# Score tiles of an attention kernel made by four 32x32 products instead of one 32x128 product

## The chip, the cores and the metric

The kernel runs on one core of one Trainium2 chip. Five engines work side by side on it: TensorE (PE, matrix products, with its weight loads shown as PEld), VectorE (DVE), ScalarE (ACT), GpSimd (POOL) and SyncE (SP, which issues the DMAs). The metric is the device time of one execution in microseconds. The kernel before takes 734.96 us, the median of three runs from 733.4 to 735.26 us.

A product on PE has a stationary operand, which a weight load puts into the array, and a moving operand that streams through it. A row of the profile gives the part of the array that a product uses as rows*columns: "32*128" has 32 rows of contraction and 128 output partitions, "128*21" has 128 rows and 21 output partitions. A product that uses less than the whole array is given a position in it (`tp`, a row and a column), and products at different positions can run at the same time. Products write to PSUM, which has eight banks of 128 partitions x 512 float32.

## The reference, cut to what matters

Two blocks of the same size stand side by side, S = 2048 rows, D = 640, 32 heads of 20 elements. Block A is softmax attention, block B is linear attention; their outputs are concatenated.

```
# A
scores = einsum("bhqd,bhkd->bhqk", q, k) * 20 ** -0.5
p = softmax(scores)
o = einsum("bhqk,bhkd->bhqd", p, v);  a = o @ wo
# B
phi(t) = where(t > 0, t + 1, exp(t)) + 1e-6
kv = einsum("bhsd,bhse->bhde", phi(k), v);  z = sum_s phi(k)
o = (phi(q) @ kv) / (phi(q) @ z + 1e-6);  b = o @ wo
out = concat(a, b)
```

The change touches only `scores` of block A.

## The kernel before, in words

**Tiling.** A unit of block A's work is a pair of a chunk of 512 queries and a group of four heads, 32 units in all (`od`). The four heads of a group lie in four strips of 32 partitions (20 elements of a head, a row for a constant, the rest unused) of `f_KT` (keys) and `f_Qr` (queries). For a unit, a block of 128 keys `kt` and a head `i` of the group, one product makes a score tile, 128 keys x 512 queries, in one PSUM bank: contraction over the 32 partitions of strip `i`, 128 output partitions. There are 32 x 16 x 4 = 2048 such tiles.

**What becomes of a tile.** Most tiles go in pairs to ACT, which takes the exponential of two banks with one instruction (L1832) and writes `f_PT`. The others go one by one to DVE, which clamps and converts them to 16-bit integers in `f_Sr` (L1730); these bits are read as bfloat16 numbers, and POOL moves them on by a constant with an integer add (L1903) twice, so that three slightly shifted approximations of the exponential are summed. The next products, of `f_PT` or `f_Sr` with the values `f_V` (or `f_Vp`, scaled), accumulate the attention output: four heads at a time, each a product of 128 rows and 21 columns at its own column position, one "quad".

**Banks.** Two pairs of banks, (0, 1) and (2, 3), take the tiles for ACT in turn; bank 4 accumulates the output (`PVB`); banks 5, 6 and 7 serve everything else: the tiles for DVE, the projections of block A and all of block B.

**Order of the work.** The whole program is written out by a planner before it runs. `_Fast.run` keeps a free time for each engine and a time at which each buffer is ready, and always lets the engine that is free first take its next step. For PE, `try_pe` tries in this order: a score burst (`try_burst`), a step of a projection or of block B that is under way, a quad of attention outputs (`try_pv`), a burst of tiles for DVE alone (`d_burst`), another step, and a small product on zeros as a filler. A score burst holds the two tiles of the next ACT instruction and, when the planner wants one and a bank is free, one tile for DVE, in rare cases two; the tiles of a burst for different heads lie in different row strips of the array. Only the last product of a burst raises the semaphore.

**Costs in the planner.** `burst` adds the given duration to PE's free time, and 107 ns (`SW`) whenever the kind of burst changes: "R" is a score burst, "C" a quad of products with 128 rows and at most 32 columns, "F" a transpose on the whole array. A score burst is given 219 ns, a quad of 512 columns 217 ns. Steps of block B are let in by the share of score bursts already placed (`pace`, `frac`). So these durations decide the order of the instructions on every engine, but not how long the chip takes for them.

**Where the diff acts.** `score_mm` makes the description of the product; `try_burst` and `d_burst` collect the tiles and hand them to `burst`. All of PE's products but the transposes are recorded at line L156, so the profile tells them apart by their tiles.

Of the kernel before, what the change touches and what calls it, by code (L numbers as in the profile page):

```python
# [769 lines left out]
class _Fast:  # L770
# [911 lines left out]

    def score_mm(self, n, kt, i, b):
        g = self.od[n][1]
        return dict(out=self.ps[:, b, :], l=self.KT[32 * i:32 * i + 32, g, 128 * kt:128 * (kt + 1)],
                    r=self.Qr[32 * i:32 * i + 32, n % 4, :], start=True, stop=True,
                    reads=self.kres(n, kt, i), writes=(("ps", b),), tp=(32 * i, 0))

    def scored(self, n):
        self.scnt[n] = self.scnt.get(n, 0) + 1  # L1690
# [52 lines left out]
    def try_burst(self, t):  # L1743
        if self.jS >= len(self.groups):
            if self.dS < len(self.dq) and self.abank:
                return self.d_burst(t)
            return False
        j = self.jS
        if j > self.jE + 1:
            return False  # L1750
        grp = self.groups[j]
        for u, n, kt, i in grp:
            if not self.kready(n, kt):
                return False
        bs = self.SB[j % len(self.SB)]
        mms = [self.score_mm(n, kt, i, bs[k]) for k, (u, n, kt, i) in enumerate(grp)]
        rd = [r for m in mms for r in m["reads"]]
        wr = [r for m in mms for r in m["writes"]]
        if self.est("pe", rd, wr) > t + 30:
            return False  # L1760
        rows = set(g[3] for g in grp)
        post = []
        want = self.dlead() < self.DLEAD and self.dfl < self.DMAX
        slack = self.free["act"] - t - 560
        if want:
            b = min(self.abank, key=lambda x: self.est("pe", (), (("ps", x),))) if self.abank else None
            pd = self.pick_d(rows, t)
            if pd is not None and (b is None or self.est("pe", (), (("ps", b),)) > t + 30):
                if slack > 0 and self.ready_c(t):
                    return False  # L1770
                pd = None
            if pd is not None:
                mm, ps_ = self.take_d(pd[0], pd[1], b)
                mms.append(mm)
                post.append(ps_)
                rows.add(pd[1])
                if self.dlead() < self.DOUBLE and self.abank and self.dfl < self.DMAX:
                    b = min(self.abank, key=lambda x: self.est("pe", (), (("ps", x),)))
                    pd = self.pick_d(rows, t) if self.est("pe", (), (("ps", b),)) <= t + 30 else None
                    if pd is not None:  # L1780
                        mm, ps_ = self.take_d(pd[0], pd[1], b)
                        mms.append(mm)
                        post.append(ps_)
        for u, n, kt, i in grp:
            self.scored(n)
        self.burst("R", mms, 219.0)
        for f in post:
            f()
        self.jS += 1
        self.q["act"].append(self.exp_op(j))  # L1790
        return True
# [4 lines left out]
    def d_burst(self, t):  # L1796
        mms, post, rows = [], [], set()
        for b in list(self.abank):
            if self.est("pe", (), (("ps", b),)) > t + 30:
                continue  # L1800
            pd = self.pick_d(rows, t)
            if pd is None:
                break
            mm, p = self.take_d(pd[0], pd[1], b)
            rows.add(pd[1])
            mms.append(mm)
            post.append(p)
        if not mms:
            return False
        self.burst("R", mms, 219.0)  # L1810
        for f in post:
            f()
        return True
# [510 lines left out]
```

## Time and profile before

| What | Value |
|---|---|
| Median of three runs | 734.96 us |
| Profiled execution, its own time | 732.96 us |
| Span of the profiled execution | 731.2 us |
| PE busy | 712.0 us, 11241 products |
| ACT busy | 694.5 us, 784 instructions |
| DVE busy | 636.9 us |
| POOL busy | 340.9 us |
| Granted PE clock, mean | 0.998 |

The busy time of PE is the union of the time from the start of each product to its modelled end. Products are pipelined: a product of 512 columns shows about 0.38 us, but the next one at the same position starts after some 0.22 us. So the distance between starts, in the timeline, tells more about PE than its busy time. A row of a timeline gives the start in us, the length in us from the first start to the last end, the engine, the line, the operation and its tiles, the array part and the moving operand, and how many instructions are merged in it. "The chain of waits" is the chain of work that ended last, followed back from the end of the span.

### The profile page before, as it was taken

How to read it: one execution, taken by the hardware profiler on the slowest of the kernel's cores; microseconds unless marked ns; L12 is line 12 of the kernel's file. 1: busy time of each engine (PE TensorE's matmuls, PEld its weight loads, DVE VectorE, ACT ScalarE, POOL GpSimd, SP SyncE). 2: the span in 40 equal slices, each digit the busy share in tenths (PEclk: the TensorE clock that was granted, in tenths of full speed). 3: DMA queues.
4: the chain of work that ended last, by engine and by line, in shares of the span. 5: the costliest groups of instructions: out<-in, count | busy, mean ns of one | idle time of the engine just before them, and what ended most of it. 6: DMA issues, size and time to landing. Idle time of an engine off the chain costs nothing.

```text
span 731.2 us, 25772 instructions
## 1 busy us (share of the span) xinstructions
PE 712.0 (97%) x11241; PEld 253.3 (35%) x11241; DVE 636.9 (87%) x1181; ACT 694.5 (95%) x784; POOL 340.9 (47%) x331
## 2 busy tenths in 40 slices
PE   8999999999999999999999999999999999999997
PEld 5323434333223333333333333323323333332333
DVE  6898888988888988898999998899889899898993
ACT  4799898999999999999999999999999999999994
POOL 7644444545554554342554443654441554424442
PEclk9999999999999999999999999999999999999999
DMA  8511011006200100102001000302102001000001
GB/s 200 157 29 35 13 33 37 13 9 151 59 10 29 32 12 18 34 4 37 20 17 34 18 9 5 101 6 47 38 15 66 23 21 35 9 27 24 6 20 59
DMA packets 42608, 27.64 MB, mean 38 GB/s; under 512 B 26890, under 2 KB 41930, under 8 KB 42490
## 3 DMA queue, kind: packets, MB, share of 16 engines
q1 hardware_dynamic: 41178, 25.62, 13.4%
q8 instruction: 89, 1.46, 0.8%
q10 hardware_dynamic: 1312, 0.33, 0.2%
q14 instruction: 29, 0.24, 0.1%
HBM read 8.40 MB, written 5.24 MB: 19 GB/s over the span
## 4 chain that ended last, share of the span: by engine, by line
PE 53%; ACT 33%; DVE 9%; POOL 1%; DMA 1%; issue 1%; SPq 0%; DVEq 0%; POOLq 0%; ACTq 0%
PE ps L156 53%; ACT f_PT L1832 32%; DVE f_Sr L1730 4%; ACT f_ar L1383 1%; POOL f_Sr L1903 1%; DVE f_T L1923 1%; DVE f_ar L1385 1%; DMA f_ar<-in_A_wqkv_dram 1%; DVE f_T L1930 1%; PE ps L1002 1%; DVE f_ar L1387 1%; DVE f_sq L1211 0%; DVE f_OTn L1927 0%; DVE f_xT L1161 0%; DVE f_Rt L1921 0%
## 5 line engine op out<-in xcount | busy, mean ns | idle before, releaser
L1832 ACT ACTIVATE f_PT<-ps 128x1024 bf16<-128x1024 f32 x724 | 681.0, 1090 | 22.7 <-PE ps L156 21.7
L1903 POOL INT64_ADD f_Sr<-f_Sr x300 | 317.4, 1067 | 370.0 <-PE ps L156 314.7
L1730 DVE TENSOR_SCALAR f_Sr<-ps 128x512 int16<-128x512 f32 x600 | 404.8, 683 | 64.1 <-PE ps L156 57.8
L156 PE MATMUL ps<-f_Qr,f_KT 32*128 32x512 bf16 x2048 | 291.7, 385 | 6.4 <-ACT f_PT L1832 3.0
L156 PEld LDWEIGHTS ps<-f_Qr,f_KT 32*128 32x128 bf16 x2048 | 73.9, 91 | 248.2 <-ACT f_PT L1832 204.6
L156 PE MATMUL ps<-f_ar 128*32 128x320 bf16 (+4 forms) x3024 | 150.1, 295 | 1.1 <-DVE f_Sr L1730 0.5
L156 PE MATMUL ps<-f_PT,f_V 128*21 128x512 bf16 x1448 | 137.2, 382 | 1.3 <-issue 1.3
L156 PE MATMUL ps<-f_Sr,f_V 128*21 128x512 bf16 x1200 | 111.0, 382 | 2.6 <-POOL f_Sr L1903 2.2
L156 PEld LDWEIGHTS ps<-f_ar 128*32 128x32 bf16 x3024 | 60.9, 95 | 61.6 <-issue 35.3
L156 PE MATMUL ps<-f_Sr,f_Vp 128*21 128x512 bf16 x600 | 58.9, 383 | 0.1
L156 PEld LDWEIGHTS ps<-f_PT,f_V 128*21 128x21 bf16 x1448 | 35.5, 90 | 42.3 <-issue 35.1
L156 PEld LDWEIGHTS ps<-f_Sr,f_V 128*21 128x21 bf16 x1200 | 28.6, 90 | 38.7 <-issue 20.0
L156 PE MATMUL ps<-f_ar,f_xT 128*32 128x160 bf16 x1280 | 34.9, 234 | 0.7 <-DMA f_ar<-in_A_wqkv_dram 0.7
L987 DVE CAST f_st<-ps 128x320 bf16<-128x320 f32 x60 | 28.3, 476 | 7.5 <-PE ps L156 7.5
L1923 DVE TENSOR_TENSOR f_T<-f_T,f_Rt 128x512 bf16<-128x512 f32 x32 | 34.3, 1071 | 0.2
L156 PE MATMUL ps<-f_wo,f_OTd 128*32 128x320 bf16 (+1 forms) x608 | 31.3, 302 | 0.0
L1383 ACT ACTIVATE f_ar<-ps 128x320 bf16<-128x320 f32 (+1 forms) x52 | 31.0, 597 | 0.0
L156 PE MATMUL ps<-f_xT,f_ar 128*32 128x512 bf16 x400 | 30.6, 382 | 0.1
L1387 DVE SCALAR_TENSOR_TENSOR f_ar<-ps,f_ar 128x320 bf16<-128x320 f32 (+1 forms) x52 | 28.8, 554 | 0.5
L156 PEld LDWEIGHTS ps<-f_ar,f_xT 128*32 128x32 bf16 x1280 | 22.9, 96 | 14.9 <-issue 9.3
L1385 DVE TENSOR_SCALAR f_ar<-f_ar 128x320 bf16<-128x320 bf16 (+1 forms) x52 | 23.3, 448 | 4.7 <-ACT f_ar L1383 3.8
L1930 DVE STREAM_TRANSPOSE f_T<-ps 128x512 f32<-128x512 f32 x32 | 22.6, 707 | 3.5 <-PE ps L156 3.5
(70 smaller groups left out, 291.1 us busy)
## 6 DMA issues: line engine op xcount, KB each, us to landing
out_dram<-f_st SPq DMA_DIRECT2D x32, 160.0 KB
f_ar<-in_B_wqkv_dram SPq DMA_DIRECT2D x3, 800.0 KB
f_OTd<-f_OTn SPq DMA_DIRECT2D x105, 20.0 KB
f_Qr<-f_sq SPq DMA_DIRECT2D x88, 20.0 KB
f_KT<-f_ar SPq DMA_DIRECT2D x22, 80.0 KB
f_ar<-in_A_wqkv_dram SPq DMA_DIRECT2D x2, 800.0 KB
f_wq<-in_A_wqkv_dram SPq DMA_DIRECT2D x1, 800.0 KB
f_wo<-in_A_wo_dram SPq DMA_DIRECT2D x1, 800.0 KB
```

The source lines that it names most:

```text
L156: lambda e: e.matmul(out, lhsT, rhs, start=start, stop=stop, tile_position=tp, skip_group_check=sgc),
L987: (lambda e: e.tensor_copy(sl, ps[:, b, 0:320])), (("ps", b),), (("stage", s, h),),
L1002: self.sch.op("pe", lambda e, m=m: e.transpose(m["out"], m["in"], m["id"]), reads=m["reads"], writes=m["writes"], inc=m.get("inc", k == le ...
L1383: self.push("act", lambda e: e.activation(r1, src, AF.Exp), (("ps", b),), (rk,), _c_act(n), prio=0, ok=ok, after=lambda: self.push("dve", ...
L1385: "dve", lambda e: e.tensor_scalar(r1, r1, 1.0, 1e-6, op0=ALU.min, op1=ALU.add), (rk,), (rk,),
L1387: "dve", lambda e: e.scalar_tensor_tensor(dst, src, 0.0, r1, op0=ALU.max, op1=ALU.add),
L1730: post = lambda: self.push("dve", lambda e: e.tensor_scalar(self.Sr[:, s, i, :], self.ps[:, b, :], 0.0, 32639.0 - self.PH[-1], op0=ALU.max ...
L1832: return _Op("act", lambda e: e.activation(self.PT[:, s0:s0 + n, :], ps[:, b0:b0 + n, :], AF.Exp, scale=math.log(2.0) / 128.0, bias=self.l ...
L1903: self.q["pool"].append(_Op("pool", lambda e: e.int64_add(v, v, inc), res, res, self.C64, self.C64 + 150, 0, self.seq, after))
L1923: "dve", lambda e: e.tensor_tensor(T2v, Tv, R.unsqueeze(2).broadcast_to([128, 16, 32]), op=ALU.mult),
L1930: self.push("dve", lambda e: e.transpose(self.T[:], ps[:, b, :]), (("ps", b),), ("T",), 630, prio=-1, after=freed, ok=lambda: n == 0 or (" ...
```

## The change

The product of a tile, 32 rows x 128 columns, is split into four of 32 rows x 32 columns. Product `j` has keys 32j to 32j+31 of the block as its weights, sits at row 32i and column 32j of the array, and writes partitions 32j to 32j+31 of the same bank. The moving operand is the same for all four. `weave` puts the products of a burst in order: first `j` = 0 of every tile, then `j` = 1 of every tile, and so on. So the 2048 products and weight loads of the scores become 8192 of each. Buffers, banks, waits between engines and all other products stay as they are. The planner is told 208 + 14 ns for each tile of the burst in place of 219 ns (222, 236, 250 and 264 ns for one to four tiles), and 107 ns for a change of kind as before; the whole order is planned anew with these numbers.

```
     def score_mm(self, n, kt, i, b):
         g = self.od[n][1]
-        return dict(out=self.ps[:, b, :], l=self.KT[32 * i:32 * i + 32, g, 128 * kt:128 * (kt + 1)],
-                    r=self.Qr[32 * i:32 * i + 32, n % 4, :], start=True, stop=True,
-                    reads=self.kres(n, kt, i), writes=(("ps", b),), tp=(32 * i, 0))
+        return [dict(out=self.ps[32 * j:32 * j + 32, b, :],
+                     l=self.KT[32 * i:32 * i + 32, g, 128 * kt + 32 * j:128 * kt + 32 * j + 32],
+                     r=self.Qr[32 * i:32 * i + 32, n % 4, :], start=True, stop=True,
+                     reads=self.kres(n, kt, i), writes=(("ps", b),), tp=(32 * i, 32 * j)) for j in range(4)]
+
+    @staticmethod
+    def weave(tiles):
+        return [m for x in zip(*tiles) for m in x]
...
-        rd = [r for m in mms for r in m["reads"]]
-        wr = [r for m in mms for r in m["writes"]]
+        rd = [r for x in mms for r in x[0]["reads"]]
+        wr = [r for x in mms for r in x[0]["writes"]]
...
-        self.burst("R", mms, 219.0)
+        self.burst("R", self.weave(mms), 208.0 + 14.0 * len(mms))
...
-        self.burst("R", mms, 219.0)
+        self.burst("R", self.weave(mms), 208.0 + 14.0 * len(mms))
```

## The prediction

> **What bounds the kernel now.** I read the busy times and the chain of waits first, then the busy time of each engine by stretch, then the chain in order of time.
>
> ```profile
> PE 712.0 (97%) x11241; PEld 253.3 (35%) x11241; DVE 636.9 (87%) x1181; ACT 694.5 (95%) x784; POOL 340.9 (47%) x331
> ...
> PE 53%; ACT 33%; DVE 9%; POOL 1%; DMA 1%; issue 1%; SPq 0%; DVEq 0%; POOLq 0%; ACTq 0%
> ```
>
> Two engines are nearly full, and the chain changes between them. The busy time by stretch says where each is full (columns: stretch, its length, then PE, PEld, DVE, ACT, POOL busy, the granted clock and DMA):
>
> ```profile
> 0.00:60.00 60.00, 56.62 (x945) 23.96 (x949) 47.78 (x90) 45.49 (x51) 35.38 (x35) 1.00 0.51 126
> 60.00:173.00 113.00, 112.52 (x2096) 42.55 (x2092) 97.12 (x171) 106.78 (x116) 53.67 (x51) 1.00 0.10 23
> 173.00:300.00 127.00, 123.00 (x1755) 40.90 (x1752) 113.00 (x196) 126.36 (x145) 62.23 (x60) 1.00 0.18 44
> 300.00:680.00 380.00, 375.25 (x5704) 126.88 (x5692) 342.11 (x643) 375.88 (x432) 172.19 (x170) 1.00 0.10 27
> 680.00:732.00 52.00, 44.65 (x772) 19.02 (x764) 36.92 (x84) 39.98 (x46) 17.41 (x17) 0.97 0.09 30
> ```
>
> From 60 to 173 us PE alone sets the pace: 0.48 us idle, while ACT idles 6.2. From 173 to 300 it is ACT (0.64 us idle, PE 4.0). From 300 to 680 both are full: PE idles 4.75 us, ACT 4.1. The granted clock is 1.00 up to 680 us, so PE can't be sped up by its clock. The chain in order of time (start, length, what) agrees:
>
> ```profile
> 69.31 63.19 PE ps L156 x1196
> 202.00 45.17 ACT f_PT L1832 x49
> 414.63 31.95 PE ps L156 x522
> ```
>
> So work that is added to PE is paid in full in the second stretch, hidden in the third as far as PE idles there, and paid in the fourth beyond 4.75 us.
>
> **The change part by part.** The rows of the groups count the tiles:
>
> ```profile
> L1832 ACT ACTIVATE f_PT<-ps 128x1024 bf16<-128x1024 f32 x724 | 681.0, 1090 | 22.7 <-PE ps L156 21.7
> L1730 DVE TENSOR_SCALAR f_Sr<-ps 128x512 int16<-128x512 f32 x600 | 404.8, 683 | 64.1 <-PE ps L156 57.8
> L156 PE MATMUL ps<-f_Qr,f_KT 32*128 32x512 bf16 x2048 | 291.7, 385 | 6.4 <-ACT f_PT L1832 3.0
> ```
>
> 724 exponentials of two tiles and 600 tiles for DVE make the 2048 products, so a score burst comes once per exponential, with 2048/724 = 2.8 tiles. Now one stretch of the timeline:
>
> ```profile
> 303.32 0.39 PE L156 MATMUL ps<-f_Qr,f_KT 32*128 32x512 bf16 x3
> 303.64 0.40 PE L156 MATMUL ps<-f_Sr,f_V 128*21 128x512 bf16 x4
> 303.65 0.10 PEld L156 LDWEIGHTS ps<-f_PT,f_V 128*21 128x21 bf16 x4
> 303.86 0.39 PE L156 MATMUL ps<-f_PT,f_V 128*21 128x512 bf16 x4
> 304.18 0.39 PE L156 MATMUL ps<-f_Qr,f_KT 32*128 32x512 bf16 x2
> ```
>
> From one quad to the next it is 0.22 us (303.64 to 303.86), but 0.32 us from the burst to the quad (303.32 to 303.64) and 0.32 us from a quad to the burst (303.86 to 304.18). So each change between the two kinds costs 0.10 us, twice per burst, and three tiles at three row strips cost no more than two.
>
> *The products.* The 512 columns of a tile still stream once; the four parts of a tile run together, like the four products of a quad. What is added is the time until the last of them has started. The products of a quad show how close together such starts are:
>
> ```profile
> 300.54 0.11 PEld L156 LDWEIGHTS ps<-f_Sr,f_V 128*21 128x21 bf16 x8 [0.23 <-issue]
> ...
> L156 PEld LDWEIGHTS ps<-f_Sr,f_V 128*21 128x21 bf16 x1200 | 28.6, 90 | 38.7 <-issue 20.0
> ```
>
> Eight weight loads, interleaved with products, take 0.11 us together where one takes 0.09 us: 0.02/7, about 3 ns from pair to pair. A tile gets three pairs more, so 9 ns; a burst of three gets 27 ns; 2048 tiles get 18.4 us of PE time. Bounds: below, 0, if the added starts overlap entirely; above, the densest supply of short products,
>
> ```profile
> 505.69 0.51 PE L156 MATMUL ps<-f_ar 128*32 128x147 bf16 x24
> 506.03 0.42 PE L156 MATMUL ps<-f_PT,f_V 128*21 128x512 bf16 x4
> ```
>
> 24 pairs in 0.34 us, 14 ns each, 43 ns per tile, 87 us in all. That row is filled by its 147 columns and not by the starts, so I stay at the first, which is a release after a change of kind just like the burst's. The Trainium skill ("TensorE: Matmul & The Clock Gate", section "Measured speedup vs the span model") gives some 4 ns per further tile of the array; by that estimate the added time would be 24.6 us, and by the same sum as below the kernel would take about 750 us; the trace's 3 ns is a little under it.
>
> *The weight loads.* 6144 more, each for 32 columns. They stand in the 3 ns of the pair. Loads of the next quad start 0.01 us after the products of the last one (303.65 against 303.64), so loads don't wait for products of the same rows; without this cover a burst would pay as in the fourth rival.
>
> *The change of kind.* A burst before differs from a quad in rows and columns, one after only in rows (32 against 128). What a change in one of the two costs is seen at the transposes, which use 128 rows and 128 columns:
>
> ```profile
> 503.69 0.45 PE L1002 MATMUL ps<-f_id,f_ar 128*128 128x128 bf16 x5
> 504.07 0.40 PE L156 MATMUL ps<-f_Sr,f_Vp 128*21 128x512 bf16 x4
> ...
> 520.56 0.45 PE L1002 MATMUL ps<-f_id,f_ar 128*128 128x128 bf16 x5
> 520.94 0.39 PE L156 MATMUL ps<-f_Qr,f_KT 32*128 32x512 bf16 x2
> ...
> L1002 PE MATMUL ps<-f_id,f_ar 128*128 128x128 bf16 x100 | 9.7, 222 | 0.0
> ```
>
> Five transposes take 0.45 us and one 0.222, so their pitch is 0.23/4 = 0.057 us and five stream for 0.285 us. To the next burst (only the rows change) and to the next quad (only the columns change) it is 0.38 us: 0.095 us over, both times, as much as where both change. So I leave both changes of a burst at 0.10 us. Bounds: as dear as now, or nothing, which is the first rival.
>
> *Waits.* None is added. Behind the burst's first round of products (`j` = 0 of each tile) stand three more, so if the bank of the DVE tile comes late, the rest of the ACT tiles is late with it; but the semaphore was raised by the burst's last product before too. ACT gets each burst 27 ns later. That is covered by the other pair of banks, whose exponential runs 0.92 us (45.17/49 in the chain); uncovered, 724 x 27 ns is 20 us, the same time as PE's and not to be added to it.
>
> *Supply of instructions.* 12288 more on PE. Priced by the queue that brings them:
>
> ```profile
> span 731.2 us, 25772 instructions
> ...
> q8 instruction: 89, 1.46, 0.8%
> ```
>
> Some 48% more instructions are about 43 packets. A packet takes 0.8% x 16 x 731.2 / 89 = 1.05 us, so uncovered they cost 45 us; but the 89 of now would be 94 us, and PE idles 19 us in all for any reason, so they are fetched ahead. I take 0.
>
> *The sum.* Where the tiles lie, by the same view for the instructions on the keys alone (the number of products stands behind PE's busy time):
>
> ```profile
> 0.00:60.00 60.00, 17.57 (x132) 4.40 (x132) 3.21 (x4) 12.96 (x7) 1.00 0.51 126
> 60.00:173.00 113.00, 46.78 (x328) 12.26 (x328) 0.00 (x0) 0.00 (x0) 1.00 0.10 23
> 173.00:300.00 127.00, 53.06 (x395) 13.30 (x392) 0.00 (x0) 0.00 (x0) 1.00 0.18 44
> 300.00:680.00 380.00, 157.91 (x1091) 39.72 (x1091) 0.00 (x0) 0.00 (x0) 1.00 0.10 27
> 680.00:732.00 52.00, 16.39 (x105) 4.19 (x105) 0.00 (x0) 0.00 (x0) 0.97 0.09 30
> ```
>
> At 9 ns per tile: first stretch 1.2 us, half of it paid, since PE waits there early on for loads: 0.6. Second: 3.0, all paid. Third: 3.6 against PE's idle 4.0: 0. Fourth: 9.8 less 4.75 idle: 5.1. Last: 0.9, 0.6 of it on the chain. Together 9.3 us. The chain's share of PE gives nearly the same, 0.53 x 18.4 = 9.8 us. So 732.96 + 9.3 = 742.3 us against the profiled execution; the median of the runs is 2.0 us above that, so I forecast 744 us. The case's own range: 739 us if the fourth stretch hides everything, 754 us if nothing is hidden (735 + 18.4). The new order of the whole program, planned for bursts of 236 and 250 ns, lies inside it.
>
> **The rivals.**
>
> *1. The change of kind gets cheaper, and the kernel faster.* Burst and quad now both sit on 32 columns, and no row shows a 32*32 product beside a 128*32 one. With 1448 changes, 18.4/1448 = 13 ns less per change is where the cost is even; at nothing left, PE would gain 145 us and ACT would bound throughout. Then the idle time of ACT goes: 6.2 us in the second stretch, 4.1 in the fourth, 0.64 in the third and perhaps 2 of the 14.5 at the start, 13 us: 722 us. Against it: the two transposes' rows above. The Trainium skill ("TensorEngine Tiling (Array Packing)", section "Key Properties") says that changing the tiling mode, and not just the tile, drains the array; by that the 0.10 us stays.
>
> *2. Hidden anyway.* If ACT and DVE hold the pace in the fourth stretch and a good order absorbs the second, 735 us. For it: ACT is 99% busy in both long stretches, and 19 us of PE's span is idle. Against: PE has 0.48 us idle in 113 us of the second.
>
> *3. Supply of instructions or starts fall behind.* At the upper bound per pair, 14 ns, 735 + 87 = 822 us; with the fetch uncovered, 735 + 45 + 9 = 789 us. Against it are the short products that run at 14 ns today, and PE's small idle time.
>
> *4. Loads that wait for products of their own rows.* Four rounds of a burst would follow each other, three more of 0.22 us for 724 bursts: 478 us, 1213 us. The Trainium skill ("TensorE: Matmul & The Clock Gate", section "The mechanism") says that a weight load overlaps products in flight only in another row group. The trace disagrees: the loads at 303.65 are for all 128 rows, and start under products in those rows.
>
> **How the numbers follow.** A measurement of this kernel tells some 0.3% from no change, 2.2 us. Forecast 68%, rival 1 14%, rival 2 12%, rival 3 4%, rival 4 2%. Faster is rival 1, same is rival 2, slower the rest, 74%. The range takes the forecast's own and rival 2 with its spread, 731 to 755 us; outside lie rivals 1, 3 and 4, 20%.
>
> **What would show it.** From the first product of a burst to the next quad: 0.32 us grows to about 0.34 to 0.35 for three tiles; 0.25 or less is rival 1, 0.45 or more rival 3, 0.98 rival 4. PE's idle time from 300 to 680 us should shrink and ACT's grow, by some 5 us; the second stretch should last about 3 us longer for the same 328 tiles. The chain should show PE over 53%. The forecast is wrong if ACT's idle time falls, or if the changes of kind cost something else than 0.10 us.

## The result and the profile after

The changed kernel takes 760.03 us, median of four runs, against 734.79 us before (four runs, one more than in the table above): a ratio of 1.0341, 95% interval 1.0306 to 1.0377. It is slower, as forecast, but by about 25 us and not by 9; 760 lies outside the range of 731 to 755. The profiled execution has a span of 755.2 us.

The burst itself does nearly what the prediction says. These are rows of the timeline of the changed kernel, and its group of score products:

```profile
303.00 0.42 PE L156 MATMUL ps<-f_Qr,f_KT 32*32 32x512 bf16 x12
303.35 0.61 PE L156 MATMUL ps<-f_xT,f_wqp 128*32 128x512 bf16 x8
303.90 0.42 PE L156 MATMUL ps<-f_Qr,f_KT 32*32 32x512 bf16 x12
...
L156 PE MATMUL ps<-f_Qr,f_KT 32*32 32x512 bf16 x8192 | 312.2, 384 | 5.5 <-ACT f_PT L1837 2.3
```

From a burst of three tiles to the next quad it is 0.35 us (303.00 to 303.35), where it was 0.32, and from the quads back to a burst the change of kind still costs some 0.1 us (303.35 to 303.90 for two quads of 0.22). All score products together are busy for 312.2 us where it was 291.7: 20.5 us more, close to the 18.4 that were forecast.

PE's share of the chain grows from 53% to 60%; that it would grow was forecast. What was not foreseen is where the time shows. The chain's shares, and the busy time in the same stretches as in the prediction (columns as there: stretch, its length, PE, PEld, DVE, ACT, POOL):

```profile
PE 60%; ACT 27%; DVE 8%; POOL 2%; DMA 1%; issue 1%; SPq 0%; DVEq 0%; POOLq 0%; ACTq 0%
...
60.00:173.00 113.00, 112.54 (x3020) 44.88 (x3016) 95.78 (x168) 103.41 (x113) 49.24 (x47) 1.00 0.11 24
173.00:300.00 127.00, 122.86 (x2768) 40.62 (x2752) 112.07 (x184) 124.05 (x140) 65.73 (x63) 1.00 0.19 40
300.00:680.00 380.00, 375.64 (x8744) 130.29 (x8734) 330.98 (x606) 376.23 (x428) 169.84 (x169) 1.00 0.11 28
680.00:756.00 76.00, 67.03 (x1570) 33.24 (x1570) 55.70 (x136) 46.55 (x57) 19.28 (x18) 0.99 0.10 33
```

From 300 to 680 us PE idles 4.36 us (4.75 before) and ACT 3.77 us (4.12 before): next to nothing was absorbed there, and ACT was not held up. After 680 us ACT is busy for 46.55 of 76 us. The end of ACT's timeline says why, first of the kernel before, then of the changed one:

```profile
705.93 13.86 ACT L1832 ACTIVATE f_PT<-ps 128x1024 bf16<-128x1024 f32 x15 [0.44 <-PE ps L156]
724.55 1.08 ACT L986 CAST f_st<-ps 128x320 bf16<-128x320 f32 x3 [4.77 <-PE ps L156]
```

```profile
700.05 22.41 ACT L1837 ACTIVATE f_PT<-ps 128x1024 bf16<-128x1024 f32 x24
726.52 0.75 ACT L986 CAST f_st<-ps 128x320 bf16<-128x320 f32 x2 [4.06 <-PE ps L156]
731.08 0.60 ACT L1383 ACTIVATE f_ar<-ps 128x512 bf16<-128x512 f32 x1 [3.81 <-PE ps L156]
...
735.46 0.60 ACT L1383 ACTIVATE f_ar<-ps 128x512 bf16<-128x512 f32 x1 [0.48 <-PE ps L156]
749.78 0.43 ACT L986 CAST f_st<-ps 128x320 bf16<-128x320 f32 x1 [13.73 <-PE ps L156]
```

The last exponential of block A ends at 719.8 us before (705.93 + 13.86) and at 722.5 us after (700.05 + 22.41): 2.7 us later. But five activations of block B (L1383; two of the five rows are shown) come behind it, and the kernel ends 32.7 us after the last exponential, not 11.4 us after it. Cut there, the changed kernel has these two stretches:

```profile
0.00:722.50 722.50, 709.82 (x16740) 255.31 (x16740) 619.40 (x1115) 691.38 (x775) 341.06 (x331) 1.00 0.15 37
722.50:755.20 32.70, 25.41 (x670) 18.68 (x662) 23.11 (x66) 4.59 (x9) 0.00 (x0) 0.99 0.18 60
```

670 products stand in the second stretch. In the kernel before it is 178:

```profile
0.00:719.80 719.80, 705.89 (x11071) 248.84 (x11075) 632.14 (x1168) 692.99 (x780) 340.74 (x331) 1.00 0.14 37
719.80:731.20 11.40, 6.16 (x178) 4.47 (x170) 4.78 (x13) 1.51 (x4) 0.15 (x1) 0.88 0.19 66
```

So nearly all of the loss, 21.3 of the 24.0 us between the two spans, is a part of block B that is left over when block A's scores are done, with ACT and POOL all but idle beside it.

### The profile page after: what moved, and what is told of

Read it like the earlier page. It is cut to its first block, busy times and chain, and to the rows that moved or that the text cites. A ratio compares the mean times of both kernels' runs of the same rounds, so it can differ in the third digit from the quotient of the medians.

```text
span 755.2 us, 38073 instructions
## 1 busy us (share of the span) xinstructions
PE 735.2 (97%) x17402; PEld 274.0 (36%) x17402; DVE 642.5 (85%) x1181; ACT 696.0 (92%) x784; POOL 341.1 (45%) x331
## 4 chain that ended last, share of the span: by engine, by line
PE 60%; ACT 27%; DVE 8%; POOL 2%; DMA 1%; issue 1%; SPq 0%; DVEq 0%; POOLq 0%; ACTq 0%
PE ps L156 60%; ACT f_PT L1837 26%; DVE f_Sr L1735 3%; POOL f_Sr L1908 2%; DVE f_T L1928 1%; DVE f_ar L1385 1%; DMA f_ar<-in_A_wqkv_dram 1%; ACT f_ar L1383 1%; DVE f_T L1935 1%; DVE f_ar L1387 0%; PE ps L1002 0%; DVE f_ar L1565 0%; DVE f_st L987 0%; DVE f_OTn L1932 0%; DVE f_rd L1563 0%
## 5 line engine op out<-in xcount | busy, mean ns | idle before, releaser
L156 PE MATMUL ps<-f_Qr,f_KT 32*32 32x512 bf16 x8192 | 312.2, 384 | 5.5 <-ACT f_PT L1837 2.3
L156 PEld LDWEIGHTS ps<-f_Qr,f_KT 32*32 32x32 bf16 x8192 | 92.9, 87 | 249.6 <-ACT f_PT L1837 219.1
L156 PE MATMUL ps<-f_ar 128*32 128x320 bf16 (+4 forms) x3024 | 145.5, 295 | 3.0 <-DVE f_ar L1387 1.2
L156 PE MATMUL ps<-f_PT,f_V 128*21 128x512 bf16 x1448 | 134.9, 382 | 0.3 <-ACT f_PT L1837 0.2
L156 PEld LDWEIGHTS ps<-f_ar 128*32 128x32 bf16 x3024 | 63.6, 95 | 61.5 <-issue 33.0
L1383 ACT ACTIVATE f_ar<-ps 128x320 bf16<-128x320 f32 (+1 forms) x52 | 28.8, 553 | 5.8 <-PE ps L156 5.8
L1928 DVE TENSOR_TENSOR f_T<-f_T,f_Rt 128x512 bf16<-128x512 f32 x32 | 32.0, 1000 | 0.2
L156 PEld LDWEIGHTS ps<-f_ar,f_xT 128*32 128x32 bf16 x1280 | 22.6, 96 | 14.6 <-issue 10.2
L156 PE MATMUL ps<-f_xT,f_wq 128*32 128x512 bf16 x320 | 25.6, 384 | 0.0
```

Source lines behind the costliest of these rows:

```text
L156: lambda e: e.matmul(out, lhsT, rhs, start=start, stop=stop, tile_position=tp, skip_group_check=sgc),
L1383: self.push("act", lambda e: e.activation(r1, src, AF.Exp), (("ps", b),), (rk,), _c_act(n), prio=0, ok=ok, after=lambda: self.push("dve", ...
L1928: "dve", lambda e: e.tensor_tensor(T2v, Tv, R.unsqueeze(2).broadcast_to([128, 16, 32]), op=ALU.mult),
```

## The experiments

Two things changed at once: what the chip executes per burst, and the order of the whole program, since the planner was told other durations. Theory C: the longer bursts on the chip are what costs. Theory P: the order planned for them costs. Each can be had without the other. The kernel before ran again beside each set of experiments, at 733.02, 733.19 and 733.33 us; each difference below is against the one of its set.

**The new products in the old order.** The planner is told 219 ns as before, so all engines keep the order of the kernel before. The edit stands in both places where a score burst is handed over.

```
-        self.burst("R", self.weave(mms), 208.0 + 14.0 * len(mms))
+        self.burst("R", self.weave(mms), 219.0)
```

> The four 32x32 products per tile, but the planner is told 219 ns per burst as before, so every engine's order is that of the kernel before. Theory P (the new order, laid out for longer bursts, is what costs more than the prediction's 9 us, because it puts block B behind the last exponentials): with the old order only what PE's idle time cannot hide is paid, 742 to 747 us. Theory C (the chip's longer bursts are paid in full under any order, because PE's idle time hides nothing): 735 plus some 20 us, 752 to 758 us. Both expect 0.35 us from the first product of a three-tile burst to the next quad.

Measured: 744.53 us, ratio 1.0158 (1.0141 to 1.0175), +11.5 us. The chain, the score products, and the stretches up to the last exponential and behind it:

```profile
PE 80%; DVE 7%; ACT 6%; POOL 4%; issue 1%; DMA 1%; ACTq 0%; DVEq 0%; POOLq 0%
...
L156 PE MATMUL ps<-f_Qr,f_KT 32*32 32x512 bf16 x8192 | 310.6, 384 | 4.9 <-ACT f_PT L1837 2.4 <-DVE f_Sr L1735 1.7
...
0.00:730.90 730.90, 719.30 (x17207) 265.31 (x17211) 634.24 (x1168) 699.02 (x780) 340.52 (x331) 1.00 0.15 38
730.90:742.60 11.70, 6.40 (x186) 4.52 (x174) 4.79 (x13) 1.56 (x5) 0.39 (x1) 0.95 0.21 74
```

Here the time goes where the prediction looked for it. Score products are busy 18.9 us more (310.6 against 291.7), the last exponential comes 11.1 us later, the stretch behind it is as short as before, and PE bounds nearly all of the way, 80% of the chain. So in the old order the products cost 11.5 us, not 20, and theory C is out.

**The old products in the new order.** One 32x128 product per tile, but the planner is told the new durations, again in both places.

```
-        self.burst("R", mms, 219.0)
+        self.burst("R", mms, 208.0 + 14.0 * len(mms))
```

> One 32x128 product per tile as before, but the planner is told 208 + 14 ns per tile, so every engine's order is that of the changed kernel. Theory P: block B still stands behind the last exponentials, 747 to 755 us. Theory C: without the longer bursts next to nothing of the loss is left, 734 to 740 us. Both expect 0.32 us from a burst's first product to the next quad.

Measured: 754.31 us, ratio 1.029 (1.0273 to 1.0307), +21.3 us, with products that the chip runs exactly as before.

```profile
0.00:718.10 718.10, 698.92 (x10594) 236.30 (x10596) 616.08 (x1115) 689.24 (x775) 340.71 (x331) 1.00 0.14 36
718.10:752.10 34.00, 26.88 (x672) 19.32 (x662) 23.29 (x66) 4.60 (x10) 0.00 (x0) 0.95 0.17 58
```

The last exponential is 1.7 us earlier than in the kernel before, and the stretch behind it is 34.0 us long, with 672 products, as in the changed kernel. That stretch is the whole loss, and it comes from the order. The two effects don't add up: with the new order given, the new products cost only some 4 to 6 us more (760.03 against 754.31 us; by the ratios 1.0341 against 1.029). That order leaves PE more room: up to the last exponential PE idles 19.2 us (718.10 - 698.92) with the old products and 12.7 us (722.50 - 709.82) with the new ones, against 13.9 us in the kernel before.

**The four products of a tile one behind the other.** The order of the burst's products is the only edit.

```
-        return [m for x in zip(*tiles) for m in x]
+        return [m for x in tiles for m in x]
```

> The changed kernel, but the four products of one tile follow each other (same row strip, four column positions), then those of the next tile. If only the number of pairs counts (3 ns each): 760 us, 0.35 us from burst to quad. If a weight load waits for products in flight in its own rows (rival 4 of the prediction), the woven order hid some of it, and this one is slower by up to 0.22 us per burst or more: above 780 us.

Measured: 758.14 us, ratio 1.0334 (1.0317 to 1.0351), the same as the changed kernel within its interval. The burst of three tiles goes to the products behind it in the same time as woven, 0.35 us:

```profile
300.21 0.42 PE L156 MATMUL ps<-f_Qr,f_KT 32*32 32x512 bf16 x12
300.56 0.46 PE L156 MATMUL ps<-f_ar 128*32 128x320 bf16 x8
```

So loads and products in the same row strip, at different column positions, run together as well as those in different strips; the prediction's fourth rival is out, and `weave` buys nothing.

**Two products of 64 columns per tile**, in the old order (219 ns told).

```
-        return [dict(out=self.ps[32 * j:32 * j + 32, b, :],
-                     l=self.KT[32 * i:32 * i + 32, g, 128 * kt + 32 * j:128 * kt + 32 * j + 32],
+        return [dict(out=self.ps[64 * j:64 * j + 64, b, :],
+                     l=self.KT[32 * i:32 * i + 32, g, 128 * kt + 64 * j:128 * kt + 64 * j + 64],
...
-                     reads=self.kres(n, kt, i), writes=(("ps", b),), tp=(32 * i, 32 * j)) for j in range(4)]
+                     reads=self.kres(n, kt, i), writes=(("ps", b),), tp=(32 * i, 64 * j)) for j in range(2)]
```

> Two products of 32 rows and 64 columns per tile in place of four of 32, with the planner's 219 ns, so the order is that of the kernel before and of e1_old_order. A tile gets one pair more in place of three. If the loss goes with the number of pairs, a third of that of e1_old_order: 6 to 7 us if that one loses 20, 3 if it loses 9; burst to quad 0.33 us. If it goes with having columns split at all, the same loss as e1_old_order.

Measured: 740.37 us, ratio 1.0103 (1.0086 to 1.012), +7.4 us: two thirds of the 11.5, not one third. So neither of the two forecasts of this run held. The timeline (a burst of three tiles, then products of another kind), the group of score products, and the durations of the weight loads (minimum/median/maximum in ns), and then those loads in the first experiment:

```profile
300.40 0.41 PE L156 MATMUL ps<-f_Qr,f_KT 32*64 32x512 bf16 x6
300.75 0.73 PE L156 MATMUL ps<-f_ar 128*32 128x320 bf16 x16
...
L156 PE MATMUL ps<-f_Qr,f_KT 32*64 32x512 bf16 x4096 | 306.7, 398 | 5.2 <-ACT f_PT L1837 2.6 <-DVE f_Sr L1735 1.7
...
L156 PEld LDWEIGHTS ps<-f_Qr,f_KT x4096: 101/101/104, 10.9 to 725.0; 32*64 32x64 bf16 x196
```

```profile
L156 PEld LDWEIGHTS ps<-f_Qr,f_KT x8192: 87/87/89, 10.7 to 729.4; 32*32 32x32 bf16 x200
```

A burst of six products keeps PE for nearly as long as one of twelve: by the start times in the trace 345 ns (median) against 351, and 321 in the kernel before. Its six products start within 17 ns, where twelve take 37. But from the last of these starts to the next quad it is 328 ns, against 315 with 32 and with 128 columns, and that makes up for most of the starts that are saved. So the cost of a burst is not the number of pairs alone. With 64 columns the loads last longer (101 ns against 87) and so do the products (398 ns against 384); which of the two holds up the quad isn't shown.

**The new products in every second burst**, in the old order.

```
+        w = 32 if self.jS % 2 else 128
...
+        return [dict(out=self.ps[w * j:w * j + w, b, :],
+                     l=self.KT[32 * i:32 * i + 32, g, 128 * kt + w * j:128 * kt + w * j + w],
...
+                     reads=self.kres(n, kt, i), writes=(("ps", b),), tp=(32 * i, w * j)) for j in range(128 // w)]
```

> The order of the kernel before (219 ns told); every second score burst is made of 32x32 products, the others of 32x128 as before. Half of PE's added time, 10 us. If PE's idle time hides the first part of it, as the prediction's sum has it, 733 + 2 = 735 to 736 us. If every added time on PE is paid at the same rate, half of the 11.5 us of e1_old_order: 738 to 740 us.

Measured: 739.79 us, ratio 1.0083 (1.0059 to 1.0108), +6.5 us.

```profile
L156 PE MATMUL ps<-f_Qr,f_KT 32*32 32x512 bf16 (+1 forms) x5114 | 302.4, 384 | 7.2 <-ACT f_PT L1838 3.6 <-DVE f_Sr L1736 2.8
```

The score products take 10.7 us more (302.4 against 291.7), of which 6.5 are paid, 61%; with all bursts it was 11.5 of 18.9, also 61%; with 64 columns 7.4 of 15.0 (306.7 against 291.7), 49%. The interval of this run alone reaches from 4.3 to 7.9 us, so the rate is known only roughly, some half to two thirds. But it excludes 2 us: PE's idle time does not swallow a first part whole and then let the rest through.

**More told to the planner for ACT.** The changed kernel, with 35 ns more told for each ACT instruction, to see whether the leftover can be planned away.

```
 def _c_act(n):
-    return 0.8333 * n + 50
+    return 0.8333 * n + 85
```

> The changed kernel, with its longer bursts told to the planner, but the planner is also told 35 ns more for each ACT instruction (0.8333 n + 85 in place of + 50), so that score bursts are placed less densely and block B fits between them. In the order of PE some 540 products fewer stand behind the last score burst than in the changed kernel (48 fewer than in the kernel before). Theory P (the loss over the 11.5 us of e1_old_order is block B left behind the last burst): 742 to 748 us. Theory Q (any order but the one of the kernel before is worse by chance): 755 us or more.

Measured: 752.68 us, ratio 1.0266 (1.0247 to 1.0284).

```profile
0.00:739.90 739.90, 727.02 (x17277) 269.82 (x17281) 633.06 (x1168) 702.71 (x780) 339.67 (x331) 1.00 0.15 37
739.90:751.00 11.10, 4.78 (x134) 3.23 (x126) 4.81 (x13) 1.41 (x4) 0.00 (x0) 0.94 0.19 65
```

The leftover is gone (134 products, 11.1 us), yet the kernel is 8 us slower than the same products in the old order: the last exponential is at 739.9 us, where it was at 730.9. So 752.68 us is neither what leftover work alone would give (742 to 748) nor what a chance order was expected to give (755 or more). Leftover work alone doesn't explain the price of an order.

**Block B let in earlier.**

```
-    B0 = 0.33
-    B1 = 0.92
+    B0 = 0.28
+    B1 = 0.82
```

> The changed kernel with block B let in earlier (B0 0.28, B1 0.82 in place of 0.33, 0.92). 130 products fewer behind the last score burst than in the changed kernel. Theory P: 760 less 130 x 43 ns = 754 us; block B is not held back by its pace but by the bursts' precedence on PE, so most of the loss stays. If the pace were what holds it back: under 748 us.

Measured: 755.87 us, ratio 1.0312 (1.0294 to 1.0331), which is not clear of the changed kernel's 1.0341 (1.0306 to 1.0377).

```profile
0.00:725.40 725.40, 713.15 (x16845) 259.60 (x16849) 622.19 (x1122) 691.58 (x776) 342.00 (x331) 1.00 0.15 37
725.40:753.20 27.80, 20.39 (x554) 14.15 (x546) 19.76 (x59) 4.43 (x10) 0.00 (x0) 0.98 0.15 52
```

The stretch behind the last exponential is 4.9 us shorter (27.8 against 32.7, 554 products against 670), close to the 5.6 of the count, but the last exponential comes 2.9 us later, so the span gains 2.0 us. A pace moved by this much leaves most of the loss. That the precedence of score bursts on PE displaces block B is a reading of the planner's code; no run changes the precedence itself.

**Other orders for the old products.** One 32x128 product per tile, only the duration told per burst differs: 233, 220, 218, 205 and 195 ns.

```
-        self.burst("R", mms, 219.0)
+        self.burst("R", mms, 220.0)
```

> One 32x128 product per tile, planner told 233 ns for every burst in place of 219. 215 products more than before stand behind the last score burst; the 494 of e2_new_costs cost 21 us, 43 ns each. Theory P: 733 + 9 = 742 us, within 2. Theory Q: no relation to that count, anything from 733 to 755.

> One 32x128 product per tile, planner told 220 ns in place of 219: a control of how far a new order alone moves the time. 16 products more behind the last score burst. Theory P: 733 to 735 us. Theory Q: the order of the kernel before is a lucky one, 738 us or more.

> One 32x128 product per tile, planner told 218 ns in place of 219. If any new order loses about what e7_told_220 lost: 738 to 744 us. If e7_told_220 is an unlucky one among equals: within 2 us of 733. 81 products more than before stand behind the last score burst, at 43 ns 3.5 us.

> As e11_told_218, but told 205 ns. 8 products more than before behind the last score burst, so by that count alone 733 us; if any new order loses some 8 us, 738 to 744 us.

> As e11_told_218, but told 195 ns. 20 products fewer than before behind the last score burst, so by that count alone 732 us; if any new order loses some 8 us, 738 to 744 us; told too short a burst, the plan may also wait for PE in places, which adds to it.

The last two columns are of the profiled execution: when the last exponential ends, and how long the stretch behind it is.

| Told per burst | Median | Ratio to before (95% interval) | Last exponential | Behind it |
|---|---|---|---|---|
| 195 ns | 735.58 us | 1.0023 (1.0012 to 1.0033) | 723.0 us | 10.9 us |
| 205 ns | 737.81 us | 1.0052 (1.0034 to 1.007) | 724.9 us | 11.7 us |
| 218 ns | 738.16 us | 1.0055 (1.0033 to 1.0078) | 720.7 us | 14.6 us |
| 219 ns (the kernel before) | 733.33 us | 1 | 719.8 us | 11.4 us |
| 220 ns | 741.01 us | 1.0105 (1.0087 to 1.0123) | 727.5 us | 11.9 us |
| 233 ns | 747.2 us | 1.0185 (1.0165 to 1.0206) | 726.1 us | 19.4 us |
| 208 + 14 n (222 to 264 ns) | 754.31 us | 1.029 (1.0273 to 1.0307) | 718.1 us | 34.0 us |

Two things stand in this table. A change of a single nanosecond in what the planner is told costs 5 or 8 us: the order of the kernel before is better than every other one tried, those next to it among them. (With 195 ns the median is 2 us above it, no more than single runs of the kernel before differ among themselves, 732.76 to 735.43 us; neither forecast for that run held.) And from 220 ns on the stretch behind the last exponential grows with what is told, while the last exponential follows no such rule. With 220 ns told nothing is left over:

```profile
0.00:727.50 727.50, 712.45 (x11070) 251.53 (x11074) 632.76 (x1167) 692.57 (x780) 340.45 (x331) 1.00 0.14 37
727.50:739.40 11.90, 6.75 (x198) 4.92 (x190) 5.34 (x14) 1.55 (x5) 0.00 (x0) 0.91 0.21 74
```

The 7.7 us that the last exponential comes later (727.5 against 719.8) are lost on the way, as after the longer ACT time above. The count of leftover products, by which I expected 733 to 735 us here and 742 for 233 ns, misses this part. It does give the stretch behind the last exponential: 81 products more made it 3.2 us longer (218 ns), 215 made it 8.0 us longer (233 ns), 494 made it 22.6 us longer (208 + 14 n), 37 to 46 ns each. The run with 233 ns has one thing more: in the stretch

```profile
173.00:200.00 27.00, 25.33 (x228) 6.35 (x226) 19.32 (x30) 23.60 (x26) 13.55 (x14) 0.76 0.51 118
```

the granted clock is 0.76, so up to 6.5 us of its 14 (0.24 x 27, an estimate) is a slower PE, about as much as its last exponential comes later. All four runs of this order have a mean clock of 0.991 to 0.995, so the slow stretch seems to come with the order.

## Why the prediction was right or wrong

**The cost of a burst: right.** 9 ns per tile and 18.4 us in all were forecast; in the old order the score products show 18.9 us more, and a burst of three tiles goes from 0.32 to 0.35 us. By the start times in the trace the twelve products of a burst start within 37 ns, 3.4 ns apart. As a rule for other splits "3 ns per pair" was incomplete: with 64 columns the next quad starts 13 ns later behind the burst's last start. The Trainium skill's 4 ns per further tile ("TensorE: Matmul & The Clock Gate", section "Measured speedup vs the span model") gave an estimate of 24.6 us, a little more than these runs show.

**The change of kind: right.** It still costs about 0.1 us, so rival 1 did not happen; the trace now shows the 32*32 product beside the 128*32 one. The Trainium skill ("TensorEngine Tiling (Array Packing)", section "Key Properties") says that a change of the tiling mode drains the array; the 0.1 us that stays agrees with that, though no run shows the draining itself.

**Loads, waits, supply of instructions: right.** The unwoven order rules out rival 4. No supply stall shows: the chain gives issue 1% before and after, with 138 packets of instructions on queue q8 after and 89 before, 49 more where 43 were forecast.

**The sum by stretches: right in size, not in its working.** For an unchanged order it gave 9.3 us; measured 11.5. But it let PE's idle time hide 3.6 us in the third stretch and 4.75 us in the fourth and charged the rest in full. Half the dose should then have cost 2 us, and cost 6.5. That 9.3 came near 11.5 is in part luck. Where the rest went, the start times in the trace show in sum. From the first product of each burst to the first one of another kind behind it, PE needs 249.8 us before and 268.1 us in the old order, 18.3 more; what lies between, the same products in the same order, shrinks from 481.4 to 474.5 us. So 6.9 us of waiting were taken up there. The table of busy times shows only 2.3 of them (span less busy falls from 19.2 to 16.9 us). The other 4.6 probably lie where a product's modelled end covers a wait for the next start, which the busy time counts as work; that last step is argued.

**The step that failed** is the sentence that ends the sum: "The new order of the whole program, planned for bursts of 236 and 250 ns, lies inside it." It was given no price of its own. With the old products the new order alone costs 21.3 us, more than the whole range left above 735. It costs it in one place: the last exponential is 1.7 us earlier than in the kernel before, and 34.0 us of work stand behind it in place of 11.4. The reason is read from the planner's code and not shown by a run: `try_pe` gives score bursts precedence, so in the plan the time by which they grow is taken from block B. In the changed kernel 670 products in place of 178 are left behind the last exponential. There they run with ACT and POOL all but idle: 25.4 us of PE time in 32.7 us. Even an order with no such leftover would have had a price that the sum lacked: those told 195 to 220 ns cost 2 to 8 us, mostly by a later last exponential (205 and 220 ns) or by some leftover work (218 ns). What the prediction said of the stretch from 300 to 680 us was wrong as well: it took added PE time to hold up the exponentials (ACT's idle time to grow by 5 us), and the last of them was only 2.7 us late in the end. By the prediction's own test, "the forecast is wrong if ACT's idle time falls", it was: 4.12 us became 3.77.

The mark of the second stretch (3 us longer for the same tiles) held, as far as it goes: 113 us bring 320 tiles (1280/4) in place of 328,

```profile
60.00:173.00 113.00, 47.99 (x1280) 14.66 (x1280) 0.00 (x0) 0.00 (x0) 1.00 0.11 24
```

eight tiles, or 8/328 x 113 = 2.8 us. But this doesn't tell the two causes apart, since both act there.

What makes one order some 5 us better than its neighbours when nothing is left over stays open. For 220 ns the trace gives a part: PE changes between kinds of product 1469 times in place of 1448, 21 changes more at 0.10 us each, and the granted clock is 0.50 for 3.4 us (177.4 to 180.8 us), up to 1.7 us; together that is at most half of the 7.7.

## What to carry to other kernels

When a program's order is written out by a planner with told durations, an edit of a duration is an edit of every engine's order: price it apart from what the chip does, by running the old work in the new order and the new work in the old one. A plan that gives one stream precedence turns a longer cost of that stream into a tail of the other; look at what stands behind the last instruction of the bounding engine. And idle time in a busy table is not a buffer that is used up first: on an engine that shares the bound, half the added work cost about half as much here (6.5 of 11.5 us), and not next to nothing.

## What the runs showed that was not expected

A weight load of 32 rows and 64 columns takes 101 ns, longer than one of 32 columns (87) and than one of 128 columns (91, in the run with the old products in the new order),

```profile
L156 PEld LDWEIGHTS ps<-f_Qr,f_KT x2048: 90/91/94, 10.6 to 716.3; 32*128 32x128 bf16 x187
```

so the length does not simply grow with the columns. The Trainium skill ("TensorE: Matmul & The Clock Gate", section "Weight-path perf modes — Fast Weight Load (FWL) and DoubleRow") says that a faster load is used when the number of weights is 128; the three durations agree with that, though no run shows the faster load itself.
